# Attention backward on one core: dK and the transpose of dS from one product per chunk, in a pair of PSUM banks of their own

## The chip, the core and the metric

The kernel runs on one core of a Trainium2 chip. The metric is device time in microseconds (us) of one execution. Three executions of the kernel before took 1696.48, 1707.16 and 1713.74 us; the median, 1707.16 us, is the time to compare with. Engines are named as in the profile: PE is the matrix engine (PEld its weight loads), DVE the vector engine, ACT the scalar engine, POOL the general one, SP the queue that issues loads.

## The reference, cut to what matters

Two independent attention blocks A and B are computed, forward and backward, with bf16 inputs. For each block:

```
B, Sq, D = 8, 96, 640;  H, Sk, Dh = 32, 512, 128
q = (x @ wq).reshape(B, Sq, H, Dh).transpose(0, 2, 1, 3)
scores = einsum("bhqd,bhkd->bhqk", q, k_cache) * Dh ** -0.5
p = softmax(scores);  o = einsum("bhqk,bhkd->bhqd", p, v_cache)
out = o.transpose(0, 2, 1, 3).reshape(B, Sq, H * Dh) @ wo
```

The outputs are the two `out`, side by side, and the gradients of all ten inputs for a given `grad_out`: dx, dK, dV, dwq and dwo of each block. With dP = dO Vᵀ, the softmax's gradient is dS = P ∘ (dP − rowsum(O ∘ dO)), and from it dK = dSᵀ Q and dQ = dS K.

## The kernel before, in words

The unit of work is a chunk: one (block, head, batch) triple, of which there are 2 × 32 × 8 = 512. A chunk has 96 query rows and 512 keys, cut into KC = 4 pieces of 128 keys. Each chunk goes through stages that lie in different ticks, one new chunk per tick, so that a tick works on about seven chunks at once. Within a tick PE's work is written in this order:

- `c_s8`, first part (L340): dQ of an older chunk, four products with `dST_sb`, into the tile `x_ps`.
- `c_s8`, second part (L346): the four pieces of the younger chunk's `dS_sb`, 96 by 128 each, are transposed by products with the identity into `dst_ps` (bf16); DVE copies that to `dST_sb` (L348). The next tick's L340 reads it.
- `c_s7` (L432): dK, four products of the same pieces of `dS_sb` with Q (`Qnat_h`, 96 by 128 a batch), into `dK_ps` (f32, one bank); ACT copies it to `dK_sb` (L435).
- `c_s45`: O (L359) and the transpose of P (L365), into the same `x_ps` as dQ; ACT takes both O and dQ out at L375 and the transpose of P (`PT_sb`) at L378.
- `c_s4`: dV (L389), taken out by ACT (L392).
- `c_s6`: dP (L417) and the row sums (`dl_ps`, L419); DVE forms `dS_sb` from both (L421).
- Scores for a younger chunk (`S_ps`, L298), with the row maximum on DVE (`negm`, L300) and the exponential on ACT (`E_sb`, L310). On DVE `rinv` (L320) and on POOL `P_sb` (L329) follow.
- For some chunks K is transposed on PE (`kT_ps`, L285) and copied by DVE (`KT_pe`, L287); for the others by a DMA.

Once a head come larger pieces: the transposes of wo and wq (`woT_ps` L210, `wqT_ps` L216), Q and dO (`q_ps`, L243), their transposes (`n_ps`, L258, copied to `Qnat_h` and `dOnat_h`), the transposes of O and dQ (`nat_ps`, L455, copied to `Onat` on ACT and `dQnat` on DVE), dwo (L470), dwq (L490). Once in a group of about six heads come the output projections `o_ps` (L512), 12 pairs of sums.

All PSUM tiles come from one pool of eight banks (`ps`, L648), handed out in turn under the tag "bank". A tile's first product waits until the engine that emptied the bank's former tile has finished. The order of instructions on each engine is made when the program is built: the emitter sorts by tick and slot, and a scheduler then orders each engine's instructions by readiness and priority. Every engine works through its own list in order.

Of the kernel before, what the change touches and what calls it, by code (L numbers as in the profile page):

```python
# [7 lines left out]
ACT = mybir.ActivationFunctionType  # L8
ALU = mybir.AluOpType
AX = mybir.AxisListType  # L10
F32 = mybir.dt.float32
BF16 = mybir.dt.bfloat16
PSUM = bass.MemoryType.PSUM
# [33 lines left out]
EV = dict(pB0="act", pB1="dve", pC00="act", pC01="act", pC10="act", pC11="dve", pD0="dve", pD1="dve", qA0="act", qA1="dve", qB0="act", qB1="dve", qD="dve", gU="act")  # L47
# [3 lines left out]
SLOTS = dict(LOAD=0, S2A=5, S2B=5.5, S1=6, S8=10, S7=20, S5=30, S4=40, S6=50, S3A=52, S3B=53, S5B=54, HEAD=SL_HEAD, GRP=SL_GRP)  # L51


def build_block(tc, em, tick0, blk, x, kc, vc, wq, wo, g_all, out_all, dx, dk, dv, dwq, dwo, ident, ones, pools, HG=6, first=True, groups=None):
    nc = tc.nc
    B, Sq, D = x.shape
    _, H, Sk, Dh = kc.shape
# [5 lines left out]
    KC = Sk // 128  # L63
    NB = 2
    assert B % NB == 0 and H % 2 == 0
    scale = float(Dh) ** -0.5
# [8 lines left out]
    t0 = 0  # L75
    while t0 < T:
        w = 512 if T - t0 >= 512 else (256 if T - t0 >= 256 else (128 if T - t0 >= 128 else T - t0))
# [3 lines left out]
    c0 = 0  # L81
    while c0 < D:
        w = 512 if D - c0 >= 512 else (256 if D - c0 >= 256 else 128)
# [12 lines left out]
    const, ps, kvp, wk, hd, hst, grp = (pools[k] for k in ("const", "ps", "kvp", "wk", "hd", "hst", "grp"))  # L96

    def bank(shape, dt, name):
        return ps.tile(shape, dt, name=name, tag="bank")

    S = {}
    G = {}
    SB = {}
    HS = pools["HS"]
    CS = pools["CS"]
# [16 lines left out]
    def setup_T(which_, t):  # L122
        def f():
            key = "xT" if which_ == 0 else "gT"
            if t == 0:
                S[key] = const.tile([128, DC, T], BF16, name=key, bufs=1)
            dst = S[key]
            if first:
                tmp = S["x_nat" if which_ == 0 else "g_nat"][:, t, :]
            else:  # L130
                tmp = S.pop(("tmp", which_, t))
            pt = bank([128, DC * 128], BF16, "tp_ps")
            for c in range(DC):
                nc.tensor.transpose(pt[:, c * 128:(c + 1) * 128], tmp[:, c * 128:(c + 1) * 128], ident[:])
            evac("act" if first and t % 2 == 0 else "dve", dst[:, :, t * 128:(t + 1) * 128], pt[:].rearrange("p (c k) -> p c k", k=128))
        return f
# [18 lines left out]
    def evac(eng, dst, src, sc=None):  # L155
        if eng == "act":
            nc.scalar.activation(dst, src, ACT.Identity, scale=(1.0 if sc is None else sc))
        else:
            if sc is None:
                nc.vector.tensor_copy(dst, src)  # L160
            else:
                nc.vector.tensor_scalar(dst, src, float(sc), None, op0=ALU.mult)
# [84 lines left out]
    def pD(h, which):  # L247
        def f():
            st = HS[(blk, h)]
            src = st["QT_h"] if which == 0 else st["dOT_h"]  # L250
            dst = hd.tile([Sq, B * 128], BF16, name="Qnat_h" if which == 0 else "dOnat_h")
            st["Qnat_h" if which == 0 else "dOnat_h"] = dst
            for b0 in range(0, B, 8):
                nb = min(8, B - b0)
                n_ps = bank([Sq, 8 * 128], BF16, "n_ps")
                for i in range(nb):
                    b = b0 + i
                    nc.tensor.transpose(n_ps[:, i * 128:(i + 1) * 128], src[:, b * Sq:(b + 1) * Sq], ident[:])  # L258
                evac(EV["pD%d" % which], dst[:, b0 * 128:(b0 + nb) * 128], n_ps[:, 0:nb * 128])
        return f  # L260

    def c_ld(h, b, n, bufs):
# [67 lines left out]
                st["P_sb"] = P_sb  # L330
        return f

    def c_s8(tick, k8, k7):
        def f():
            XP[tick] = bank([128, 1024], BF16, "x_ps")
            if k8 is not None:
                st = CS[(k8[0], k8[1], k8[2])]
                dQT_ps = XP[tick][:, 2 * Sq:4 * Sq].bitcast(F32)
                for c in range(KC):
                    nc.tensor.matmul(dQT_ps, st["K_sb"][:, c, :], st["dST_sb"][:, c * Sq:(c + 1) * Sq], start=(c == 0), stop=(c == KC - 1))  # L340
                del CS[(k8[0], k8[1], k8[2])]
            if k7 is not None:
                st7 = CS[(k7[0], k7[1], k7[2])]
                dST_ps = bank([128, KC * Sq], BF16, "dst_ps")
                for c in range(KC):
                    nc.tensor.transpose(dST_ps[:, c * Sq:(c + 1) * Sq], st7["dS_sb"][:, c * 128:(c + 1) * 128], ident[0:Sq, 0:Sq])  # L346
                dST_sb = wk.tile([128, KC * Sq], BF16, name="dST_sb", bufs=2)
                nc.vector.tensor_copy(dST_sb[:], dST_ps[:])  # L348
                st7["dST_sb"] = dST_sb
        return f  # L350

    def c_s45(tick, k8, k5, k4):
# [72 lines left out]
    def c_s7(h, b):  # L425
        def f():
            st = CS[(blk, h, b)]
            hs = HS[(blk, h)]
            dS_sb = st["dS_sb"]
            dK_ps = bank([128, KC * 128], F32, "dK_ps")  # L430
            for c in range(KC):
                nc.tensor.matmul(dK_ps[:, c * 128:(c + 1) * 128], dS_sb[:, c * 128:(c + 1) * 128], hs["Qnat_h"][:, b * 128:(b + 1) * 128], start=True, stop=True)  # L432
            if b % 2 == 0:
                SB[(blk, h, b // 2, "k")] = wk.tile([128, 2, KC * 128], BF16, name="dK_sb", bufs=3)
            nc.scalar.activation(SB[(blk, h, b // 2, "k")][:, b % 2], dK_ps[:], ACT.Identity, scale=1.0)  # L435
        return f

    def qA(h, which):
# [113 lines left out]
    for g in range(NG):  # L552
        h0 = GH0[g]
        for hh in range(groups[g]):
            h = h0 + hh
# [56 lines left out]
        for i, (which, t, gi) in enumerate(subs):  # L612
            if which == 0:
                tk = cLg + OFF["s5"] + 2 + (i * gs0) // n_out
            else:
                tk = cLg + OFF["s8"] + 2 + gs0 - 3 + ((i - n_out) * gs1) // n_out
# [6 lines left out]
def _kernel_impl(tc, A_x, A_k_cache, A_v_cache, A_wq, A_wo, B_x, B_k_cache, B_v_cache, B_wq, B_wo, grad_out,  # L623
           out_0, out_1, out_2, out_3, out_4, out_5, out_6, out_7, out_8, out_9, out_10, HG=6, slots=None, off=None, hk=None, ev=None, gspread=None, groupsA=None, groupsB=(6, 6, 6, 6, 6, 2)):
    global GSPREAD0, GSPREAD1
    nc = tc.nc
    if slots:
        SLOTS.update(slots)
    if off:
        OFF.update(off)  # L630
    if hk:
        HK.update(hk)
    if ev:
        EV.update(ev)
    if gspread:
        GSPREAD0, GSPREAD1 = gspread
    with ExitStack() as ctx:
        P = lambda **kw: ctx.enter_context(tc.tile_pool(**kw))
        cst = P(name="gconst", bufs=1)
        ident = cst.tile([128, 128], BF16, name="ident")  # L640
        make_identity(nc, ident[:])
        ones = cst.tile([128, 1], BF16, name="ones")
        nc.vector.memset(ones[:], 1.0)
        warm = cst.tile([128, 128], BF16, name="warm")
        nc.vector.memset(warm[:], 1.0)
        pools = dict(
            const=P(name="const", bufs=1),
            ps=P(name="ps", bufs=8, space=PSUM),  # L648
            kvp=P(name="kv", bufs=11),
            wk=P(name="wk", bufs=3),  # L650
            hd=P(name="hd", bufs=2),
            hst=P(name="hst", bufs=HG + 2),
            grp=P(name="grp", bufs=1),
            stp=P(name="stp", bufs=5),
        )
        warm_ps = pools["ps"].tile([128, 128], F32, name="warm_ps", tag="bank")
        for _ in range(32):
            nc.tensor.matmul(warm_ps[:], warm[:], warm[:], start=True, stop=True)
        pools["SX"] = {}
        pools["XP"] = {}  # L660
        pools["OD"] = pools["const"].tile([128, 2, HG + 2, A_x.shape[0] * A_x.shape[1]], BF16, name="OD", bufs=1)
        pools["HS"] = {}
        pools["CS"] = {}
        em = Emitter()
        t_next = 13
        for blk, args in enumerate(((A_x, A_k_cache, A_v_cache, A_wq, A_wo, grad_out, out_0, out_1, out_2, out_3, out_4, out_5),
                                    (B_x, B_k_cache, B_v_cache, B_wq, B_wo, grad_out, out_0, out_6, out_7, out_8, out_9, out_10))):
            H_ = args[1].shape[1]
            if blk == 0:
                grps = groupsA  # L670
            else:
                grps = groupsB
            t_next = build_block(tc, em, t_next, blk, *args, ident, ones, pools, HG=HG, first=(blk == 0), groups=grps)
        for tk, (k8, k7, k5, k4) in pools["SX"].items():
            em.add(tk, SLOTS["S8"], pools["c_s8"](tk, k8, k7))
            em.add(tk, SLOTS["S5"], pools["c_s45"](tk, k8, k5, k4))
        em.run()

# [63 lines left out]
```

## Time and profile before

| what | value |
|---|---|
| executions, us | 1696.48, 1707.16, 1713.74 |
| profiled execution, first to last instruction (span), us | 1699.8 |
| PE busy | 1675.7 us, 99% |
| DVE busy | 1329.8 us, 78% |
| ACT busy | 1405.2 us, 83% |
| POOL busy | 1040.3 us, 61% |
| granted PE clock, mean | 0.998 |
| `dst_ps` transposes (L346) | 2048 |
| dK products (L432) | 2048 |
| copy of `dst_ps` by DVE (L348) | 512, 346 ns each |
| copy of `dK_ps` by ACT (L435) | 512, 590 ns each |

The profile gives the span; the time of the profiled execution, which has what lies around the span in it too, is not recorded apart from the three above. The span is 7.4 us under their median. A busy time is the union of an engine's instructions; products overlap each other, so a row's mean duration is longer than the step from one product's start to the next one's. In the timeline "x4" joins four instructions, and the difference of two rows' starts is the time that PE really gave to the first.

### The profile page before, as it was taken

What the parts mean: (1) busy time and instruction counts of PE and PEld (TensorE: products, weight loads), DVE (VectorE), ACT (ScalarE), POOL (GpSimd) and SP (SyncE); (2) the same over time, 40 slices, a digit from 0 to 9 for tenths busy, and PEclk for the clock granted to TensorE, in tenths of its full rate; (3) what the DMA queues carried; (4) which work ended last, traced back from release to release, by engine and by line L of the source; (5) the groups of instructions that cost most, each with busy time, mean ns of one, the idle gap of its engine ahead of it and who ended that gap; (6) DMA issues with size and microseconds to landing.
All of it is one profiled execution on the core that took longest, in us unless ns stands there. A gap on an engine that the chain in (4) does not pass through costs nothing.

```text
span 1699.8 us, 56567 instructions
## 1 busy us (share of the span) xinstructions
PE 1675.7 (99%) x22024; PEld 1343.8 (79%) x22024; DVE 1329.8 (78%) x3052; ACT 1405.2 (83%) x3518; POOL 1040.3 (61%) x1747
## 2 busy tenths in 40 slices
PE   8999999999999999999999999999999999999999
PEld 7877778778778778777778877887788778778876
DVE  6887678878788878787778876787788778878877
ACT  6998889869869869878768998897799679878975
POOL 3676567646647647656566764675576557656754
PEclk9999999999999999999999999999999999999999
DMA  9999999999999999999999999999899989999994
GB/s 256 252 259 250 258 225 260 262 242 243 262 221 252 268 238 259 225 251 237 281 256 269 273 270 248 238 289 248 218 261 276 237 221 261 281 217 240 263 247 141
DMA packets 600429, 423.05 MB, mean 249 GB/s; under 512 B 419360, under 2 KB 557984, under 8 KB 600160
## 3 DMA queue, kind: packets, MB, share of 16 engines
q1 hardware_dynamic: 546576, 242.08, 72.2%
q0 software_dynamic: 53584, 177.35, 32.7%
q8 instruction: 173, 2.83, 0.7%
q14 instruction: 96, 0.79, 0.2%
HBM read 161.09 MB, written 159.12 MB: 188 GB/s over the span
## 4 chain that ended last, share of the span: by engine, by line
PE 89%; DMA 4%; ACT 3%; issue 1%; DVE 1%; POOL 0%; SPq 0%; DVEq 0%; ACTq 0%; POOLq 0%
PE q_ps L243 12%; PE o_ps L512 12%; PE dwo_ps L470 6%; PE dV_ps L389 6%; PE dK_ps L432 6%; PE S_ps L298 6%; PE dP_ps L417 6%; PE dwq_ps L490 6%; PE x_ps L340 5%; PE x_ps L365 5%; PE dst_ps L346 5%; PE x_ps L359 5%; PE kT_ps L285 3%; PE n_ps L258 3%; PE nat_ps L455 2%; DMA VT<-V_sb 1%
## 5 line engine op out<-in xcount | busy, mean ns | idle before, releaser
L329 POOL TENSOR_SCALAR P_sb<-E_sb,rinv 96x512 bf16<-96x512 bf16 x512 | 352.6, 689 | 567.8 <-DVE rinv L320 559.2
L310 ACT ACTIVATE E_sb<-S_ps,negm 96x512 bf16<-96x512 f32 x512 | 351.0, 686 | 187.6 <-DVE negm L300 181.9
L421 DVE SCALAR_TENSOR_TENSOR dS_sb<-dP_ps,dl_ps,P_sb 96x512 bf16<-96x512 f32 x512 | 382.1, 746 | 60.9 <-PE dl_ps L419 54.6
L300 DVE TENSOR_REDUCE negm<-S_ps 96x1 f32<-96x512 f32 x512 | 347.6, 679 | 50.9 <-PE S_ps L298 46.6
L435 ACT ACTIVATE dK_sb<-dK_ps 128x512 bf16<-128x512 f32 x512 | 302.1, 590 | 63.4 <-PE dK_ps L432 56.5
L392 ACT ACTIVATE dV_sb<-dV_ps 128x512 bf16<-128x512 f32 x512 | 311.6, 609 | 0.0
L378 ACT ACTIVATE PT_sb<-x_ps 128x384 bf16<-128x384 bf16 x512 | 253.1, 494 | 0.0
L512 PEld LDWEIGHTS <-OD 128*128 128x128 bf16 x1536 | 132.2, 98 | 100.4 <-issue 1.0
L398 POOL DMA_DIRECT2D out_dram<-dV_sb x256 | 194.9, 761 | 11.8 <-issue 8.6
L398 POOL DMA_DIRECT2D out_dram<-dK_sb x256 | 195.0, 762 | 9.1 <-issue 4.4
L389 PE MATMUL dV_ps<-dOnat_h,P_sb 96*128 96x128 bf16 x2048 | 198.2, 219 | 0.8 <-DVE dOnat_h L160 0.6
L417 PE MATMUL dP_ps<-VT,dOT_h 128*96 128x512 bf16 x512 | 195.4, 382 | 3.0 <-DMA VT<-V_sb 3.0
L432 PE MATMUL dK_ps<-Qnat_h,dS_sb 96*128 96x128 bf16 x2048 | 198.1, 219 | 0.1
L407 POOL TENSOR_TENSOR prod<-OD,dOT_h 128x96 bf16<-128x96 bf16 x512 | 184.2, 360 | 13.8 <-ACT OD L375 12.6
L348 DVE COPY dST_sb<-dst_ps 128x384 bf16<-128x384 bf16 x512 | 177.1, 346 | 10.5 <-PE dst_ps L346 10.3
L365 PE MATMUL x_ps<-ident,P_sb 96*128 96x96 bf16 x2048 | 172.0, 205 | 0.8 <-POOL P_sb L329 0.3
L359 PE MATMUL x_ps<-PT_sb,V_sb 128*128 128x96 bf16 x2048 | 172.3, 206 | 0.2 <-ACT PT_sb L378 0.2
L346 PE MATMUL dst_ps<-ident,dS_sb 96*128 96x96 bf16 x2048 | 172.3, 206 | 0.2 <-DVE dS_sb L421 0.2
L340 PE MATMUL x_ps<-dST_sb,K_sb 128*128 128x96 bf16 x2048 | 171.0, 206 | 1.3 <-ACT dK_sb L435 0.8
L375 ACT ACTIVATE OD<-x_ps 128x192 bf16<-128x192 f32 (+1 forms) x515 | 167.9, 326 | 3.9 <-PE x_ps L340 3.9
L320 DVE RECIPROCAL rinv<-rowsum 96x1 f32<-96x1 f32 x512 | 79.9, 156 | 106.0 <-ACT E_sb L310 100.4
L340 PEld LDWEIGHTS <-K_sb 128*128 128x128 bf16 x2048 | 131.1, 98 | 25.1 <-issue 1.6
(84 smaller groups left out, 3744.4 us busy)
## 6 DMA issues: line engine op xcount, KB each, us to landing
out_dram<-dV_sb POOLq DMA_DIRECT2D x256, 256.0 KB, 5.2
out_dram<-dK_sb POOLq DMA_DIRECT2D x256, 256.0 KB, 5.3
K_sb<-in_A_k_cache_dram SPq DMA_DIRECT2D x128, 256.0 KB, 5.3
V_sb<-in_A_v_cache_dram SPq DMA_DIRECT2D x128, 256.0 KB, 5.2
K_sb<-in_B_k_cache_dram SPq DMA_DIRECT2D x128, 256.0 KB, 5.0
V_sb<-in_B_v_cache_dram SPq DMA_DIRECT2D x128, 256.0 KB, 4.9
out_dram<-dwo_sb POOLq DMA_DIRECT2D x63, 160.0 KB, 4.8
out_dram<-dwq_sb POOLq DMA_DIRECT2D x31, 320.0 KB, 6.1
```

The lines of the kernel that those rows point to most:

```text
L300: nc.vector.tensor_reduce(negm[:], S_ps[:], axis=AX.X, op=ALU.max, negate=True)
L310: nc.scalar.activation(E_sb[:], st["S_ps"][:], ACT.Exp, bias=st["negm"][:], scale=1.0, accum_out=rowsum[:])
L329: pinned(nc.gpsimd.tensor_scalar(P_sb[:], st["E_sb"][:], st["rinv"][:], 0.0, op0=ALU.mult, op1=ALU.add))
L340: nc.tensor.matmul(dQT_ps, st["K_sb"][:, c, :], st["dST_sb"][:, c * Sq:(c + 1) * Sq], start=(c == 0), stop=(c == KC - 1))
L389: nc.tensor.matmul(dV_ps[:, c * 128:(c + 1) * 128], P_sb[:, c * 128:(c + 1) * 128], hs["dOnat_h"][:, b * 128:(b + 1) * 128], start=True, s ...
L392: nc.scalar.activation(SB[(blk, h, b // 2, "v")][:, b % 2], dV_ps[:], ACT.Identity, scale=1.0)
L398: pinned(nc.gpsimd.dma_start(dst[b - 1:b + 1, h].rearrange("b (p c) d -> p b (c d)", c=KC), SB.pop((blk, h, b // 2, which))[:]))
L417: nc.tensor.matmul(dP_ps[:], hs["dOT_h"][:, tok], st["VT"], start=True, stop=True)
L421: nc.vector.scalar_tensor_tensor(dS_sb[:], dP_ps[:], dl_ps[:, 0:1], st["P_sb"][:], op0=ALU.subtract, op1=ALU.mult)
L432: nc.tensor.matmul(dK_ps[:, c * 128:(c + 1) * 128], dS_sb[:, c * 128:(c + 1) * 128], hs["Qnat_h"][:, b * 128:(b + 1) * 128], start=True, s ...
L435: nc.scalar.activation(SB[(blk, h, b // 2, "k")][:, b % 2], dK_ps[:], ACT.Identity, scale=1.0)
L512: nc.tensor.matmul(o_ps[:], src[:, t * 128:(t + 1) * 128], rhs, start=(hh == 0), stop=(hh == groups[g] - 1))
```

## The change

The transpose of dS is no longer a product of its own. Q and a 96 by 96 identity stand side by side in a new constant tile `QN`, so that one product of a piece of `dS_sb` with 224 columns gives both dK's piece (128 columns) and the transpose's (96). Even and odd batches share one identity: Q of the even batch, identity, Q of the odd batch. `QN` has two slots, used by heads in turn, and the identities are written once at the start. The result is f32 and needs two banks: a tile `dk_pair` in a pool slot of its own, one buffer of two banks; the other tiles have six banks in place of eight. DVE copies the transpose from the pair (f32 now, in four runs) to `dST_sb`, then ACT copies dK's four runs to `dK_sb`. In the program as built, ACT's copy waits for DVE's. The copy of Q into `QN` (`pD`) writes runs of 128 columns.

```
-            if k7 is not None:
-                dST_ps = bank([128, KC * Sq], BF16, "dst_ps")
-                for c in range(KC):
-                    nc.tensor.transpose(dST_ps[:, c * Sq:(c + 1) * Sq], st7["dS_sb"][:, c * 128:(c + 1) * 128], ident[0:Sq, 0:Sq])
-                dST_sb = wk.tile([128, KC * Sq], BF16, name="dST_sb", bufs=2)
-                nc.vector.tensor_copy(dST_sb[:], dST_ps[:])
-                st7["dST_sb"] = dST_sb
...
-            dK_ps = bank([128, KC * 128], F32, "dK_ps")
+            rhs = nat_view(pools["QN"], hs["nslot"], b)
+            pair = ps.tile([128, 2, 512], F32, name="dk_pair", tag="pair", bufs=1)
             for c in range(KC):
-                nc.tensor.matmul(dK_ps[:, c * 128:(c + 1) * 128], dS_sb[:, c * 128:(c + 1) * 128], hs["Qnat_h"][:, b * 128:(b + 1) * 128], start=True, stop=True)
+                nc.tensor.matmul(pair[:, c // 2, (c % 2) * (128 + Sq):(c % 2 + 1) * (128 + Sq)], dS_sb[:, c * 128:(c + 1) * 128], rhs, start=True, stop=True)
+            k0, t0 = (0, 128) if b % 2 == 0 else (Sq, 0)
+            dST_sb = wk.tile([128, KC * Sq], BF16, name="dST_sb", bufs=2)
+            nc.vector.tensor_copy(in4(dST_sb[:]), pair_part(pair, t0, Sq))
+            st["dST_sb"] = dST_sb
...
-            nc.scalar.activation(SB[(blk, h, b // 2, "k")][:, b % 2], dK_ps[:], ACT.Identity, scale=1.0)
+            nc.scalar.activation(in4(SB[(blk, h, b // 2, "k")][:, b % 2]), pair_part(pair, k0, 128), ACT.Identity, scale=1.0)
...
-            ps=P(name="ps", bufs=8, space=PSUM),
+            ps=P(name="ps", bufs=6, space=PSUM),
...
+    def nat_view(t, slot, b):
+        return t[:, slot, b // 2, 0:128 + Sq] if b % 2 == 0 else t[:, slot, b // 2, 128:256 + Sq]
+
+    def pair_part(pair, c0, w):
+        return pair[:, :, 0:2 * (128 + Sq)].rearrange("p a (c n) -> p a c n", c=2)[:, :, :, c0:c0 + w]
...
+            if which == 0:
+                st["nslot"] = (blk * H + h) % 2
+                v = pools["QN"][:, st["nslot"], 0, 0:128]
+                v = bass.AP(v.tensor, v.offset, [v.ap[0], (256 + Sq, B // 2), (128 + Sq, 2), (1, 128)])
+                evac(EV["pD0"], v, n_ps[:].rearrange("p (a c n) -> p a c n", c=2, n=128))
...
+        pools["QN"] = pools["const"].tile([sq, 2, nb // 2, 256 + sq], BF16, name="QN", bufs=1)
+        for s_ in range(2):
+            for p_ in range(nb // 2):
+                nc.vector.tensor_copy(pools["QN"][:, s_, p_, 128:128 + sq], ident[0:sq, 0:sq])
```

The order as built also changes. Before, ACT's list within a tick is E, dK, O/dQ, PT, dV in 449 of the 512 ticks. After, dK's copy stands third in 141 of the ticks (E, O/dQ, dK, PT, dV), fourth in 217 (E, O/dQ, PT, dK, dV) and fifth or later in about 145; in 63 of these it stands behind a head's copy as well (`Onat`, `woT_h` or `dwo_sb`). On PE the new product stands where the transposes stood in 421 ticks, behind O and the transpose of P in 41, behind dV in 22 and behind dP in 20.

More of the change, by code (lines that the diff above doesn't have):

```diff
@@ L99, in bank, with in4 @@
         return ps.tile(shape, dt, name=name, tag="bank")
+    def nat_view(t, slot, b):
+        return t[:, slot, b // 2, 0:128 + Sq] if b % 2 == 0 else t[:, slot, b // 2, 128:256 + Sq]
+    def pair_part(pair, c0, w):
+        return pair[:, :, 0:2 * (128 + Sq)].rearrange("p a (c n) -> p a c n", c=2)[:, :, :, c0:c0 + w]
+    def in4(ap):
+        return ap.rearrange("p (a c n) -> p a c n", a=2, c=2)
     S = {}
@@ L250, in f @@
             src = st["QT_h"] if which == 0 else st["dOT_h"]
[L251 to L259, printed above, removed]
+            n_ps = bank([Sq, B * 128], BF16, "n_ps")
+            for b in range(B):
+                nc.tensor.transpose(n_ps[:, b * 128:(b + 1) * 128], src[:, b * Sq:(b + 1) * Sq], ident[:])
+            if which == 0:
[3 more added lines that the diff above has]
+                evac(EV["pD0"], v, n_ps[:].rearrange("p (a c n) -> p a c n", c=2, n=128))
+            else:
+                st["dOnat_h"] = hd.tile([Sq, B * 128], BF16, name="dOnat_h")
+                evac(EV["pD1"], st["dOnat_h"][:], n_ps[:])
         return f
@@ L331, in c_s3b, with c_s8 @@
         return f
-    def c_s8(tick, k8, k7):
+    def c_s8(tick, k8):
         def f():
@@ L341, in f @@
                 del CS[(k8[0], k8[1], k8[2])]
-            if k7 is not None:
-                st7 = CS[(k7[0], k7[1], k7[2])]
-                dST_ps = bank([128, KC * Sq], BF16, "dst_ps")
-                for c in range(KC):
-                    nc.tensor.transpose(dST_ps[:, c * Sq:(c + 1) * Sq], st7["dS_sb"][:, c * 128:(c + 1) * 128], ident[0:Sq, 0:Sq])
-                dST_sb = wk.tile([128, KC * Sq], BF16, name="dST_sb", bufs=2)
-                nc.vector.tensor_copy(dST_sb[:], dST_ps[:])
-                st7["dST_sb"] = dST_sb
         return f
@@ L663, in _kernel_impl @@
         pools["CS"] = {}
+        sq, nb = A_x.shape[1], A_x.shape[0]
+        pools["QN"] = pools["const"].tile([sq, 2, nb // 2, 256 + sq], BF16, name="QN", bufs=1)
+        for s_ in range(2):
+            for p_ in range(nb // 2):
+                nc.vector.tensor_copy(pools["QN"][:, s_, p_, 128:128 + sq], ident[0:sq, 0:sq])
         em = Emitter()
@@ L674, in _kernel_impl @@
         for tk, (k8, k7, k5, k4) in pools["SX"].items():
-            em.add(tk, SLOTS["S8"], pools["c_s8"](tk, k8, k7))
+            em.add(tk, SLOTS["S8"], pools["c_s8"](tk, k8))
             em.add(tk, SLOTS["S5"], pools["c_s45"](tk, k8, k5, k4))
```

## The prediction

> **What bounds the kernel now.** I read the page first, for the share of each engine.
>
> ```profile
> PE 1675.7 (99%) x22024; PEld 1343.8 (79%) x22024; DVE 1329.8 (78%) x3052; ACT 1405.2 (83%) x3518; POOL 1040.3 (61%) x1747
> ```
>
> PE is busy 99%, but its products overlap, so I took the timeline next and measured from start to start. The four rows below are one stretch of PE in a tick.
>
> ```profile
> 269.05 0.33 PE L340 MATMUL x_ps<-dST_sb,K_sb 128*128 128x96 bf16 x4
> 269.22 0.34 PE L346 MATMUL dst_ps<-ident,dS_sb 96*128 96x96 bf16 x4
> 269.39 0.39 PE L432 MATMUL dK_ps<-Qnat_h,dS_sb 96*128 96x128 bf16 x4
> 269.62 0.34 PE L359 MATMUL x_ps<-PT_sb,V_sb 128*128 128x96 bf16 x4
> ```
>
> Four products of 96 columns step by 0.17 us (42 ns each), four of 128 by 0.22 to 0.23 (55 ns each). There is no idle time between groups and no sign of the weight loads: PE streams columns. The next rows are five products of 256 columns in another stretch, 0.54 us for five, 108 ns each.
>
> ```profile
> 803.19 0.71 PE L243 MATMUL q_ps<-xT,wq_p 128*128 128x256 bf16 x5
> ...
> 803.73 0.71 PE L243 MATMUL q_ps<-gT,woT_h 128*128 128x256 bf16 x5
> ```
>
> Then the busy times by stage, one stretch per head. Columns: stretch, its length, busy us of PE, PEld, DVE, ACT, POOL, clock, DMA share, GB/s.
>
> ```profile
> 253.60:274.80 21.20, 21.13 (x306) 17.48 (x304) 18.00 (x42) 20.98 (x55) 14.98 (x26) 1.00 1.14 282
> 274.80:299.10 24.30, 24.18 (x338) 20.37 (x335) 19.98 (x45) 21.82 (x56) 17.18 (x29) 1.00 1.13 250
> 299.10:321.80 22.70, 22.64 (x319) 18.40 (x316) 18.16 (x43) 21.51 (x55) 16.64 (x28) 1.00 1.15 269
> 321.80:353.80 32.00, 32.00 (x396) 24.73 (x393) 24.09 (x55) 22.11 (x54) 16.26 (x27) 1.00 1.14 243
> ```
>
> This is what decides. The mean of 83% for ACT hides two kinds of heads. In heads with output projections (32 us) ACT and DVE have 8 to 10 us free. In light heads (21.2 and 22.7 us) ACT is busy 99% and 95%: PE and ACT bound them together. The lengths repeat every six heads with two light ones among them, so about 21 of 64 heads are light. Everything PE needs from ACT comes late there, and eight banks of slack have hidden it so far.
>
> **The change part by part.**
>
> PE. Removed per chunk: four transposes and four dK products, 269.22 to 269.62, 0.39 to 0.40 us. Added: four products of 224 columns. Between 55 ns at 128 and 108 ns at 256, a straight line gives 55 + 53 × 96/128 = 95 ns, 0.38 us. Gain 0.01 to 0.02 us × 512, about 6 us (5 to 10). The columns streamed are the same, 4 × (96 + 128) = 4 × 224; only the step over each product's columns, some 2 ns × 2048, is saved, and 2048 weight loads that cost nothing. This is the most that PE can give, since it does not wait now.
>
> Here a rule speaks against the row. The Trainium skill, "TensorE: Matmul & The Clock Gate", section "Back-to-back issue gap", says that in streams of weight loads and products a product of 128 columns costs about 81 ns and one of 512 about 131 ns. By that, two products would cost some 160 ns, one of 224 about 94 ns, and the change would be worth an estimated 140 us. The rows above step by 55 ns at 128 columns, so I go by the rows.
>
> DVE. The copy to `dST_sb` takes 346 ns from bf16; from f32 these are the nearest rows:
>
> ```profile
> L348 DVE COPY dST_sb<-dst_ps 128x384 bf16<-128x384 bf16 x512 | 177.1, 346 | 10.5 <-PE dst_ps L346 10.3 <-PE x_ps L365 0.2
> L160 DVE CAST dwo_sb<-dwo_ps 128x320 bf16<-128x320 f32 x64 | 30.8, 481 | 0.5
> L160 DVE CAST dOT_h<-q_ps 128x256 bf16<-128x256 f32 x64 | 26.6, 415 | 8.3 <-PE q_ps L243 8.3
> ```
>
> 64 columns more cost 66 ns, so 384 columns cost 481 + 66 = 547 ns, 0.20 us more. Over 512 that is 103 us of DVE, which has 370 us idle. Light heads: 18.0 + 8 × 0.2 = 19.6 of 21.2 us. Covered on the whole; the bounds are 0 and, were nothing of it covered in the 21 light heads, 21 × 1.6 = 34 us. DVE still has 1.6 us free in such a head, so I take a quarter, 9 us. Queued behind the longer copy are `rinv`, `dS_sb` and `negm`, for which POOL, PE and ACT wait.
>
> ACT. The copy of dK keeps its 512 columns (590 ns), now in four runs from two banks. No row has that; rows of one size with and without runs on DVE agree (`xT` 128x640 482 ns, `wqT_h` 128x640 478), so 0 is taken, and the spread of ACT's two 512-column copies (590 and 609 ns, 10 us over 512) is kept as the bound on both sides. What changes is the wait: this copy is now behind DVE's, and the next tick's product behind it, since the pair has one buffer. For the why, the Trainium skill, "PSUM — Partial Sum Buffer", section "PSUM bank collisions raise a hardware error", says that two engines may not access one bank at a time, reads included. No row of this trace shows it.
>
> The wait's price is walked in a light head. ACT there:
>
> ```profile
> 269.70 0.68 ACT L310 ACTIVATE E_sb<-S_ps,negm 96x512 bf16<-96x512 f32 x1
> ...
> 270.38 0.58 ACT L435 ACTIVATE dK_sb<-dK_ps 128x512 bf16<-128x512 f32 x1
> 270.86 0.32 ACT L375 ACTIVATE OD<-x_ps 128x192 bf16<-128x192 f32 x1
> 271.07 0.49 ACT L378 ACTIVATE PT_sb<-x_ps 128x384 bf16<-128x384 bf16 x1
> 271.44 0.60 ACT L392 ACTIVATE dV_sb<-dV_ps 128x512 bf16<-128x512 f32 x1
> 271.92 0.71 ACT L157 ACTIVATE woT_h<-woT_ps 128x640 bf16<-128x640 bf16 x1
> 272.50 0.70 ACT L310 ACTIVATE E_sb<-S_ps,negm 96x512 bf16<-96x512 f32 x1
> ```
>
> and PE in the tick after:
>
> ```profile
> 271.61 0.33 PE L340 MATMUL x_ps<-dST_sb,K_sb 128*128 128x96 bf16 x4
> 271.77 0.34 PE L346 MATMUL dst_ps<-ident,dS_sb 96*128 96x96 bf16 x4
> ```
>
> ACT's steps from start to start are 0.68, 0.48 (dK), 0.21, 0.37, 0.48, 0.58. The order as built puts dK last here. So O starts at 270.38, PT at 270.59, dV at 270.96, `woT_h` at 271.44 and ends 272.15, dK at 272.02 and ends 272.60. With six banks, dQ's `x_ps` has the bank that `woT_ps` had: PE wants it at 271.61 and gets it at 272.15, 0.54 late. The new product stands behind O and the transpose of P in this tick, so it is wanted 0.51 after dQ, 272.66 by then; dK is out at 272.60. The same walk two heads' copies earlier, with `Onat` (0.82) in place of `woT_h`, gives 0.3 to 0.4 us at the tick that begins at 264.05. If ACT slips no further, the second loss has the first in it; if it slips with PE, they add. So 0.55 to 0.9 us a light head, 12 to 19 us over 21; the score product, which with six banks waits for the copy of PT (270.59 + 0.49 = 271.08 against 270.76 in this tick), is inside the first and adds where the head's copies are elsewhere. I take 0.95 a light head, 20 us, and 0.2 for each of the other 43, 9 us. Bounds: nothing, if the waits only eat slack; and 1.5 us in every head, about 95 us, if each of two or three such waits costs its own time.
>
> The eight copies of the identity at the start are 96 columns each, while DVE waits 7.1 us for the first transposes: nothing. `pD`'s copy in runs: nothing, by the two rows of 640 columns. Loads, stores and POOL's list are the same.
>
> Sum: −6 + 9 + 20 + 9 = +32 us. The profiled span is 1699.8 us, 7.4 under the median of the runs; added to the median, 1707.2 + 32 = 1739 us.
>
> **The rivals.**
>
> *The waits are hidden, and PE's gain remains* (the other side). For it: the scheduler has moved the new product behind O, dV or dP in 83 ticks, and DVE and ACT have whole microseconds free in the 43 other heads. Against it: in light heads ACT has 0.22 us in 21.2. Price: 1707 − 6 = 1701, up to 1724 if half of my waits stay. It decides if light heads lose under 0.3 us each.
>
> *Lockstep.* The loop product, DVE's copy, ACT's copy, next product (0.55 + 0.55 + 0.6 us and queueing) and the loop scores, `negm`, E, PT, bank, scores both close every tick, and a light tick has 2.4 to 2.7 us. If a delay on one engine is passed on to the next and not caught up, light heads stretch by 2 to 4 us: 21 × 3 + 43 × 1 − 6 = +100, 1807 us. For it: ACT at 99%. Against it: three quarters of all time has slack on two engines.
>
> *The product does not stream.* Two 224-column results a bank, f32, read by two engines: if it stepped like one of 256 columns, 108 ns, PE would lose 13 × 2048 = 27 us, 1766 with the rest; nothing in the rows suggests it.
>
> **How the numbers follow.** My forecast (waits of 23 to 85 us net of the gain, 1724 to 1790): 0.58. Hidden, 1690 to 1724: 0.28. Lockstep and anything above 1790: 0.11. A gain over 1%, under 1690: 0.03, since PE can give only 10. The point is the forecast's 1739. The range leaves out about a tenth on each side: 1703 (hidden, the gain alone nearly whole) to 1790. One per cent, 17 us, is about what a measurement can tell from no change: faster 0.03, same 0.28, slower 0.69.
>
> **What would show it.** PE: four products of 224 columns stepping by 0.38 us; more than 0.40 and that term is wrong. DVE: the copy near 547 ns. Light heads: 22 to 23 us in place of 21.2, with PE waits on ACT before dQ, the scores and the pair; heavy heads unchanged at 32. If light heads stay at 21.2 or shorter, the waits were hidden and I am wrong; if heavy heads grow too, it is lockstep.

## The result and the profile after

After the change the kernel takes 1760.62 us (median of four runs, 1759.78 to 1761.83), before it 1703.21 us (median of four, 1696.48 to 1713.74). The ratio is 1.032, with a 95% interval of 1.0273 to 1.0366: 57 us slower. The profiled span grew from 1699.8 to 1758.0 us.

The page of the profile after, busy times and the shares of the chain that ended last:

```profile
PE 1701.4 (97%) x19976; PEld 1342.9 (76%) x19976; DVE 1432.0 (81%) x3060; ACT 1423.1 (81%) x3518; POOL 1028.9 (59%) x1747
...
PE 65%; ACT 21%; DVE 9%; issue 5%; DMA 0%; POOL 0%; ACTq 0%; SPq 0%; DVEq 0%; POOLq 0%
```

The chain of the kernel before:

```profile
PE 89%; DMA 4%; ACT 3%; issue 1%; DVE 1%; POOL 0%; SPq 0%; DVEq 0%; ACTq 0%; POOLq 0%
```

PE's "busy" fell only from 99% to 97% and looks harmless. The chain says more: before, 89% of it was PE; now it leaves PE for ACT and DVE in 30% of the span. PE has become an engine that is waited for by others and waits for them.

The same four heads as in the prediction (stretch, length, busy us of PE, PEld, DVE, ACT, POOL):

```profile
259.00:281.60 22.60, 21.76 (x275) 17.56 (x272) 19.66 (x42) 21.54 (x55) 14.89 (x26) 1.00 1.14 270
281.60:306.40 24.80, 24.35 (x304) 20.34 (x302) 21.45 (x45) 21.94 (x55) 17.04 (x29) 1.00 1.14 258
306.40:330.60 24.20, 23.35 (x287) 18.42 (x284) 19.78 (x43) 21.84 (x55) 16.48 (x28) 1.00 1.10 278
330.60:363.70 33.10, 32.54 (x365) 24.85 (x362) 25.55 (x55) 21.96 (x54) 16.04 (x27) 1.00 1.08 218
```

They were 21.2, 24.3, 22.7 and 32.0 us. The two light heads lost 1.4 and 1.5 us, the others 0.5 and 1.1. PE had 0.07 us without a product in the first of them before, and has 0.84 now.

The timeline where a score product is late (start, duration, engine, line, tiles; in brackets the idle time and what ended it). It shows rows of PE and ACT, and last the row maximum on DVE; the dots stand for rows left out:

```profile
264.71 0.55 PE L436 MATMUL dk_pair<-QN,dS_sb 96*128 96x224 bf16 x4
...
265.09 0.34 PE L362 MATMUL x_ps<-PT_sb,V_sb 128*128 128x96 bf16 x4
...
265.98 0.31 ACT L378 ACTIVATE OD<-x_ps 128x192 bf16<-128x192 f32 x1
...
266.19 0.48 ACT L381 ACTIVATE PT_sb<-x_ps 128x384 bf16<-128x384 bf16 x1
266.24 0.22 PE L262 MATMUL n_ps<-ident,dOT_h 128*96 128x128 bf16 x1
...
266.56 0.59 ACT L443 ACTIVATE dK_sb<-dk_pair 128x512 bf16<-128x512 f32 x1
266.72 0.38 PE L309 MATMUL S_ps<-KT,QT_h 128*96 128x512 bf16 x1 [0.27 <-ACT PT_sb L381]
...
267.13 0.69 DVE L311 TENSOR_REDUCE negm<-S_ps 96x1 f32<-96x512 f32 x1 [0.21 <-PE S_ps L309]
```

Four products of 224 columns take 0.38 us from 264.71 to 265.09, as forecast. But S_ps starts 0.48 us after the 128-column product ahead of it, which needs 0.055: 0.43 us of PE are lost until `PT_sb` has been copied out of the bank, and the row maximum behind S_ps, on DVE, waits too. The bracket shows only 0.27, since the end of a product is modelled late; steps between starts show it in full.

Taken over the whole trace in that way (each step from one product's start to the next one's, less what its columns need), PE lost 49 us before and 113 us after. A loss is put down here to the copy on another engine that ended last before the product. Of these 113 us, 30 stand before S_ps behind the copy of `PT_sb` (104 times) and 22 before other tiles behind the same copy; 12 before dQ's `x_ps` behind `Onat` or `woT_h`; and 13 before the new product, 4 of them behind dK's copy and 9 behind `dS_sb`. The rest is spread over many small waits, most of which were there before. Lost time grew by some 63 us; less some 6 us that the product saves, that is about the 58 us of the span.

The three groups that the change touched:

```profile
L443 ACT ACTIVATE dK_sb<-dk_pair 128x512 bf16<-128x512 f32 x512 | 307.7, 601 | 2.0 <-DVE dST_sb L439 1.9
L436 PE MATMUL dk_pair<-QN,dS_sb 96*128 96x224 bf16 x2048 | 280.9, 259 | 3.5 <-DVE dS_sb L424 1.3
L439 DVE CAST dST_sb<-dk_pair 128x384 bf16<-128x384 f32 x512 | 280.7, 548 | 29.7 <-PE dk_pair L436 20.9 <-PE dwo_ps L478 0.3
```

ACT stood 1.9 us in all at its new wait for DVE: the wait that the change adds in plain sight costs nothing on ACT.

### The profile page after: what moved, and what is told of

The parts are those of the page before. It is cut to its first block, busy times and chain, and to the rows that moved or that the text cites. A ratio compares the mean times of both kernels' runs of the same rounds, so it can differ in the third digit from the quotient of the medians.

```text
span 1758.0 us, 52467 instructions
## 1 busy us (share of the span) xinstructions
PE 1701.4 (97%) x19976; PEld 1342.9 (76%) x19976; DVE 1432.0 (81%) x3060; ACT 1423.1 (81%) x3518; POOL 1028.9 (59%) x1747
## 4 chain that ended last, share of the span: by engine, by line
PE 65%; ACT 21%; DVE 9%; issue 5%; DMA 0%; POOL 0%; ACTq 0%; SPq 0%; DVEq 0%; POOLq 0%
PE o_ps L520 11%; PE q_ps L252 10%; ACT E_sb L321 8%; PE dk_pair L436 6%; PE dwq_ps L498 6%; PE S_ps L309 5%; DVE negm L311 5%; PE dwo_ps L478 4%; ACT PT_sb L381 4%; PE dV_ps L392 4%; PE dP_ps L420 4%; ACT dK_sb L443 3%; PE x_ps L351 3%; PE x_ps L368 3%; PE x_ps L362 3%
## 5 line engine op out<-in xcount | busy, mean ns | idle before, releaser
L424 DVE SCALAR_TENSOR_TENSOR dS_sb<-dP_ps,dl_ps,P_sb 96x512 bf16<-96x512 f32 x512 | 381.4, 745 | 22.7 <-PE dl_ps L422 11.9
L443 ACT ACTIVATE dK_sb<-dk_pair 128x512 bf16<-128x512 f32 x512 | 307.7, 601 | 2.0 <-DVE dST_sb L439 1.9
L439 DVE CAST dST_sb<-dk_pair 128x384 bf16<-128x384 f32 x512 | 280.7, 548 | 29.7 <-PE dk_pair L436 20.9
L436 PE MATMUL dk_pair<-QN,dS_sb 96*128 96x224 bf16 x2048 | 280.9, 259 | 3.5 <-DVE dS_sb L424 1.3
L381 ACT ACTIVATE PT_sb<-x_ps 128x384 bf16<-128x384 bf16 x512 | 248.6, 486 | 0.0
L436 PEld LDWEIGHTS <-dS_sb 96*128 96x128 bf16 x2048 | 171.5, 97 | 14.4 <-DVE dS_sb L424 12.6
L368 PE MATMUL x_ps<-ident,P_sb 96*128 96x96 bf16 x2048 | 178.2, 205 | 0.3
L252 PE MATMUL q_ps<-gT,woT_h 128*128 128x512 bf16 (+1 forms) x640 | 136.8, 325 | 4.7 <-ACT PT_sb L381 3.9
```

The lines of the kernel that those rows point to most:

```text
L252: nc.tensor.matmul(q_ps[:], lhs(c), rhsT[:, c, t0:t0 + w], start=(c == 0), stop=(c == DC - 1))
L381: nc.scalar.activation(PT_sb[:], PT_ps, ACT.Identity, scale=1.0)
L424: nc.vector.scalar_tensor_tensor(dS_sb[:], dP_ps[:], dl_ps[:, 0:1], st["P_sb"][:], op0=ALU.subtract, op1=ALU.mult)
L436: nc.tensor.matmul(pair[:, c // 2, (c % 2) * (128 + Sq):(c % 2 + 1) * (128 + Sq)], dS_sb[:, c * 128:(c + 1) * 128], rhs, start=True, stop= ...
L443: nc.scalar.activation(in4(SB[(blk, h, b // 2, "k")][:, b % 2]), pair_part(pair, k0, 128), ACT.Identity, scale=1.0)
```

## The experiments

My theory after the result: the loss is bank shortage. The two products need two banks at a time as before, but those two are now set apart, and the tiles that go round on the other six meet a bank whose last reader, ACT, is late. The rivals: DVE's longer copy (T2), and the chain product, DVE's copy, ACT's copy, next product, through a pair with one buffer (T3).

**The split of the banks alone.** Before, with the banks of after.

```
-dST_ps = bank([128, KC * Sq], BF16, "dst_ps")
+dST_ps = ps.tile([128, KC * Sq], BF16, name="dst_ps", tag="dst", bufs=1)
...
-dK_ps = bank([128, KC * 128], F32, "dK_ps")
+dK_ps = ps.tile([128, KC * 128], F32, name="dK_ps", tag="dk", bufs=1)
...
-ps=P(name="ps", bufs=8, space=PSUM)
+ps=P(name="ps", bufs=6, space=PSUM)
```

> The products of before, with the banks of after: the transposes of dS and dK each have one bank of their own, and six banks are left for the rest. If the shortage of banks is what costs (the score product that waits for PT_sb is the largest wait of PE in the profile after), this lies near 1745 us, at least 1730. If the longer copy on DVE or the serial chain product, DVE's copy, ACT's copy, next product is the cause, neither is here, and it stays at 1700 to 1712.

Measured 1804.4 us, ratio 1.0589 (1.0547 to 1.0632). Neither the longer copy nor the chain is in it, and it loses 100 us, more than the whole change. So split banks can cost all of it, and something in the change has won some of it back. The waits of PE in this run (engine, tile, line, releaser: us, times, longest):

```profile
PE S_ps L298 <- ACT PT_sb L378: 30.4, 97, 0.5
PE dwq_ps L490 <- ACT PT_sb L378: 11.9, 28, 0.5
PE q_ps L243 <- ACT PT_sb L378: 9.1, 14, 0.9
```

All three wait for the copy of `PT_sb`; by steps from start to start PE loses 100 us in all behind that copy here, against 53 after the change. In the order as built, ACT's copy of dK stands ahead of that of `PT_sb` in practically every tick here (in 430 of them as E, dK, O/dQ), as it did before the change, and in 146 after it; it puts `PT_sb` off by its own step of 0.48 us.

**DVE's longer copy alone.** Before, with f32 transposes.

```
-dST_ps = bank([128, KC * Sq], BF16, "dst_ps")
+dST_ps = bank([128, KC * Sq], F32, "dst_ps")
...
-nc.tensor.transpose(dST_ps[:, c * Sq:(c + 1) * Sq], st7["dS_sb"][:, c * 128:(c + 1) * 128], ident[0:Sq, 0:Sq])
+nc.tensor.matmul(dST_ps[:, c * Sq:(c + 1) * Sq], st7["dS_sb"][:, c * 128:(c + 1) * 128], ident[0:Sq, 0:Sq], start=True, stop=True)
```

> Before with one change: the transposes of dS are f32 products with the identity, so that DVE's copy takes about 548 ns in place of 346; eight banks and the order of work as before. If DVE's longer copy costs, 1735 to 1760 us. If the banks or the chain do, under 1715.

Measured 1720.84 us, ratio 1.0106 (1.0049 to 1.0163): 16 us beside the 1704.44 of its own runs of before, just above the line drawn for the theory of banks and well under T2's. The copy took 547 ns. Its cost is real: PE waits for `dS_sb`, which now comes later; by steps from start to start it loses 16 us behind `dS_sb`, against 1 us before. First the copy's row, then one of PE's waits:

```profile
L348 DVE CAST dST_sb<-dst_ps 128x384 bf16<-128x384 f32 x512 | 279.9, 547 | 10.2 <-PE dst_ps L346 9.2
...
PE dst_ps L346 <- DVE dS_sb L421: 8.8, 22, 0.7
```

**The short copy in the changed kernel.**

```
-nc.vector.tensor_copy(in4(dST_sb[:]), pair_part(pair, t0, Sq))
+nc.vector.tensor_copy(in4(dST_sb[:]), pair_part(pair, t0, Sq // 2).bitcast(BF16))
```

> After with DVE's copy reading the transpose's first halves as bf16 (384 columns of bf16, about 346 ns, as before the change; the transpose that comes out is not dS's, so dQ, dwq and dx are left wrong). If banks are the cause, 1745 to 1758 us, a small gain. If DVE's copy is the cause, 1700 to 1720.

Measured 1785.61 us, ratio 1.0488 (1.0441 to 1.0535): slower than after with less work on DVE, which no theory expected. The order as built gave it away: with the shorter copy (median 344 ns) the scheduler puts dK's copy ahead of `PT_sb`'s in 347 ticks in place of 146, presumably since it takes dK as ready earlier. The run does not tell the price of the copy, but points at the order on ACT.

**dK's copy ahead of DVE's.** The two lines of `c_s7` that copy out of the pair exchanged.

> After with ACT's copy of dK ahead of DVE's copy of the transpose: the same two copies from the same pair, the chain in the other order. If banks are the cause, within 15 us of after (1745 to 1775). If ACT's wait for DVE is the cause, 1700 to 1725.

Measured 1854.07 us, ratio 1.0883 (1.0839 to 1.0927). A miss for all: turned round, the kernel takes 93 us more. DVE's copy now waits for ACT, which is late, and dQ for DVE (rows of the waits of PE):

```profile
PE x_ps L351 <- DVE dST_sb L442: 34.6, 57, 1.2
PE S_ps L309 <- ACT PT_sb L381: 10.5, 53, 0.5
```

The 93 us need not all be the chain's: the order on ACT changed along with it, and dK's copy stands ahead of `PT_sb`'s in nearly every tick here, as in the split of the banks alone, which took 1804.4 us. But dQ's wait for DVE is new. So T3's chain can cost time; whether it does in the order that the change chose, this run does not tell.

**A bank of its own for S_ps.** If the meeting of two tiles in one bank were the loss, to keep them apart would cure it.

```
-S_ps = bank([Sq, Sk], F32, "S_ps")
+S_ps = ps.tile([Sq, Sk], F32, name="S_ps", tag="s", bufs=1)
...
-ps=P(name="ps", bufs=6, space=PSUM)
+ps=P(name="ps", bufs=5, space=PSUM)
```

> After with one of its six banks kept for the score tile S_ps alone, five for the rest. In after, 104 score products wait for ACT's copy of PT_sb, whose x_ps had their bank, 30 us in all. If that meeting of two tiles in one bank is the loss, 1715 to 1740 us. If six banks are simply too few, the waits move to the other tiles on five banks, and this is at 1755 us or more.

Measured 1953.15 us, ratio 1.1445 (1.1373 to 1.1517). The waits moved to the next tiles in turn, and became larger:

```profile
PE n_ps L262 <- ACT PT_sb L381: 51.1, 97, 0.6
PE wqT_ps L225 <- ACT PT_sb L381: 15.4, 27, 0.6
PE dl_ps L422 <- ACT PT_sb L381: 12.5, 10, 1.5
```

Keeping S_ps apart cured nothing: another tile meets the late bank. The 190 us need not all be the missing bank's, for the order on ACT changed here too: dK's copy stands ahead of `PT_sb`'s in some 430 ticks, in place of 146.

**Seven banks in place of eight.** Before, `bufs=7`, nothing else.

> Before with seven banks in its pool, the eighth unused; nothing else changed. If the number of banks for tiles that go round in turn is what counts, this loses some 15 to 40 us (1718 to 1745); if only the special banks of the change cost, it stays at 1700 to 1712.

Measured 1747.26 us, ratio 1.0241 (1.0171 to 1.0311). One bank less, with nothing else edited and nearly the same order on ACT, costs 45 us. Eight banks hid the lateness of ACT and seven do not, which PE's waits before do not show: there it waits for nearly nothing.

**dK's copy late.** After, with ACT's copy of dK written behind that of `PT_sb`.

```
+st["pair"] = pair_part(pair, k0, 128)
...
+em.add(ct + OFF["s7"], 35, c_s7k(h, b))
```

(`c_s7k` holds the copy; slot 35 lies behind the slot of `PT_sb`'s copy, 30.)

> After with ACT's copy of dK put behind that of PT_sb in every tick (in after it stands ahead of it in 146 ticks and delays it by 0.48 us there); the wait of the next product for the pair can only grow. If the score product's wait for PT_sb is the main loss, some 8 to 20 us are won: 1740 to 1753. If the chain product, DVE's copy, ACT's copy, next product is the main loss, this is slower than after: 1765 to 1785.

Measured 1735.43 us, ratio 1.0193 (1.0106 to 1.0281): 25 us faster than after (22 by the ratios; 8 to 20 were expected), though the pair is set free later. T3 falls as the main loss. Who waited for the tile `PT_sb`, after:

```profile
  PE S_ps L309: 15.3, 67
  PE q_ps L252: 7.4, 14
  PE o_ps L520: 2.5, 7
```

and with dK's copy late:

```profile
  PE q_ps L252: 4.6, 12
...
  PE S_ps L309: 0.3, 1
  PE o_ps L525: 0.3, 2
```

The bracketed idle time before S_ps is gone. By steps from start to start 15 of the 30 us there remain; behind the copy of `PT_sb` in all, 32 of 53.

**The same with the short copy.** The edits of the last run and of the short copy together.

> The same with DVE's copy at the old 346 ns (the first halves read as bf16; dQ, dwq and dx are left wrong). The run with the short copy alone took 1785.6 us, but there ACT's copy of dK stood ahead of PT_sb's in 347 ticks. If that order made it slow, this comes to 1735 to 1750; what it then lacks to the run beside it with the long copy is DVE's share (5 to 15 us). If the short copy itself is slow in some way, it stays near 1785.

Measured 1726.76 us, ratio 1.0135 (1.0064 to 1.0205), where the short copy without the late dK took 1785.61. The order made that run slow. Beside the long copy with late dK the short one is worth 9 us, a difference that the two intervals do not part from nothing.

**Two products or one, with as many banks and the same order on ACT.** The split banks with two products, and the one product in its pair, each with the order of ACT fixed to `PT_sb`, dK, dV in every tick (by `pinned(...)` around the copies of `PT_sb` and dK, for the one product of dV too).

> Two separate products and the banks of after (transposes of dS and dK one bank each, six for the rest; 1804 us with dK's copy ahead of PT_sb's in 430 ticks), now with ACT's order fixed: the copies of PT_sb, then dK, in every tick. If the order of ACT is what made that run slow, it falls by 40 to 80 us, to 1725 to 1765, and the same banks with the one product (1735 us with late dK) differ from it by under 20 us. If two products are slow in themselves on six banks, it stays above 1785.

> The one product with ACT's order fixed to PT_sb, dK, dV in every tick (1735 us with dK behind PT_sb, where 144 ticks still had dK last). If the next product's wait for the pair matters, this is faster, 1715 to 1730; if the wait of S_ps for PT_sb alone does, 1728 to 1742. ACT could also stand at DVE's copy, then 1745 or more.

Measured 1738.29 us for two products, ratio 1.0211 (1.0167 to 1.0255), and 1738.36 us for one, ratio 1.0212 (1.0175 to 1.0249). In both kernels ACT's order is E, O/dQ, `PT_sb`, dK, dV in all but a few ticks. The order on PE is not quite alike: the one product stands behind O or further back in some 45 ticks, the two products in hardly any.

With as many banks and the same order on ACT the one product is worth nothing, to within some 10 us. That DVE's longer copy takes what PE saves is likely (6 us and some 9), but these two runs do not show the parts.

The order is worth far more: two products on split banks took 1804.4 us with dK's copy ahead and take 1738.3 with it behind, 66 us less.

Two of the same four heads, first with two products, then with one:

```profile
251.40:273.10 21.70, 21.23 (x306) 17.59 (x305) 18.51 (x42) 21.22 (x55) 14.84 (x26) 1.00 1.13 254
273.10:297.80 24.70, 24.47 (x337) 20.47 (x336) 20.19 (x46) 22.05 (x55) 17.04 (x29) 1.00 1.14 276
```

```profile
253.10:275.20 22.10, 21.59 (x272) 17.60 (x271) 19.91 (x42) 21.29 (x55) 14.81 (x26) 1.00 1.11 270
275.20:299.70 24.50, 24.40 (x305) 20.42 (x303) 21.76 (x46) 22.15 (x56) 17.02 (x29) 1.00 1.13 264
```

In the light head, where DVE goes from 18.5 to 19.9 us, one product loses 0.4 us; in the next it wins 0.2. In the run with late dK, dK's place behind dV in 144 ticks cost nothing that shows: fixed ahead of dV (1738.36 us) it is no faster.

**The order alone, on eight and seven banks.** Before, and before with seven banks, with dK's copy behind `PT_sb`'s (the same edit).

> Before, eight banks, with only dK's copy put behind PT_sb's on ACT. With eight banks PE waits for neither, so by the theory of banks this changes nothing: 1695 to 1712. If the order of ACT's copies is worth something by itself, 1675 to 1690, or above 1720 if dK's bank is then late.

> Before with seven banks and dK's copy behind PT_sb's on ACT, in place of 1747 us with seven banks and dK's copy ahead. PT_sb's copy and with it x_ps's bank come 0.48 us earlier, but dK's bank 0.5 us later. Of the 45 us lost on seven banks, 13 stand at waits of S_ps for PT_sb and 25 at waits for dK's copy: if the order only moves the wait, 1735 to 1760; if PT_sb is the one that counts, 1715 to 1735.

Measured 1707.42 us on eight, ratio 1.001 (0.9977 to 1.0043), and 1751.84 us on seven, ratio 1.0299 (1.026 to 1.0338). On eight banks the order of ACT's copies is free. So the run on eight banks and the one of two products on split banks, both with dK's copy behind `PT_sb`'s, differ by their edits in the banks alone: 1707.4 and 1738.3 us. The 31 us between them are the price of the banks (2.1% against before itself).

On seven the order only moves the wait. By steps from start to start, with the steps at `q_ps` and `o_ps` left out (records of some of their products are missing from this trace), PE's losses behind dK's copy fall from 24 to 9 us, but those behind `PT_sb`'s grow from 17 to 22 and those behind DVE's copy `KT_pe` from 2 to 16. In these runs the order pays only where dK has a bank of its own.

No kernel of these beats the one before.

## Why the prediction was right, and where it was off

The time, 1760.6 us, lies 22 us above the forecast, in the forecast's own band of 1724 to 1790 and in the stated range of 1703 to 1790; slower had 0.69. The sum was +32 us and is +57. The ranges are wide, and the upper end of the band does not quite follow from its terms: waits of 85 us less the gain of 6 give 1786.

- PE's term was right. The products step by 95 ns, and the saving is about 6 us. No weight load showed itself. By the step of 81 ns at 128 columns that the Trainium skill gives ("TensorE: Matmul & The Clock Gate", "Back-to-back issue gap") the change would have won, by the prediction's estimate. The rows decide.
- DVE's term was right in the duration, 547 ns forecast and 548 measured. Its size fits: 9 us forecast, 9 us between the long and the short copy with late dK (the two intervals overlap), 16 us when it is put alone into the kernel before. That 9 meets 9 is in part luck, since the quarter behind it was a choice.
- ACT's copy of dK from four runs in two banks: 601 ns after 590, 6 us over 512 copies, inside the bound of 10.
- The waits were mis-sized: 29 us forecast, and some 54 by what the other terms leave of the 63 us of lost time, if DVE's copy takes its 9 here too. The mechanism was right, that the banks come from an ACT which is late. But the walk went by dQ's tile and the pair, and took the score product's wait for `PT_sb` to be "inside the first"; it is the main one, 30 us before S_ps and 22 before other tiles, against 13 at the pair. The walked losses are there: `Onat` 20 times with 0.36 us each (0.3 to 0.4 forecast), `woT_h` 21 times with 0.24 (0.54 forecast): 0.60 us together, where 0.55 to 0.9 was walked for a light head.
- No term of the sum was for the order on ACT, which the scheduler makes anew with each edit. It is some 20 of the 57 us.
- The term of 0.2 us for each of the other 43 heads failed most. From the dP product at one head's start to that of the next head, the 20 heads of under 23.2 us grew by 27 us together, as the terms for light heads say (20 and 9, less some 2 of PE's gain). The 43 others grew by 32 us, where 9 less some 4 was forecast.
- "Heavy heads unchanged at 32" was wrong: 33.1 us. They have the same tiles and more of them, and the copy of `PT_sb` holds back S_ps, dwq's and the projections' products there as well, however much free time ACT has on the whole. By the prediction's own sign ("if heavy heads grow too, it is lockstep") this speaks for lockstep in part; but the two light heads shown stretched by 1.4 and 1.5 us, not by 2 to 4.
- The wait that the diff shows, ACT behind DVE, cost 1.9 us.

What the runs show in its place, as a sum of ratios: six banks for the rest, with dK's copy fixed behind that of `PT_sb` on ACT, 2.1% (36 us); one product for two, 0.0%; the order on ACT that the scheduler made of the change, 1.1% (3.2% less 2.1%, some 20 us). The hidden-waits rival fell; the lockstep rival was too large at 1807 us, but the last link of its second loop (scores, `negm`, E, `PT_sb`, bank, scores), the score product's wait for the bank that `PT_sb` is copied from, is the largest wait in the trace; the rival of a product that does not stream fell.

Open: how the 36 us divide between fewer banks and banks set apart. With the same order on ACT, seven banks that all go round cost more than six and two set apart (3.0% against 2.1%). One product with eight banks for the rest would need ten, so it was not tried.

## What to carry to other kernels

Before a change takes banks from a pool, try the kernel with a pool one smaller: an engine that never waits can have no buffer to spare. Where an engine in order empties several banks, rank its copies by who waits next for each bank, and look at the order as built, not at the source: a cheaper instruction can make a slower kernel by changing the order. Merging two products into one with the same columns saves next to nothing where the rows step by columns alone, as here (some 6 us of 1700), and what matters is then the banks and the copies behind it.

## What was not expected of the hardware

- A copy by DVE of four f32 runs that lie in two banks costs no more than one run in one bank: 548 ns against 547 for 384 columns. ACT's costs 601 against 590 for 512.
- Products with a weight load each step by their columns, with no sign of the load: 42 ns at 96 columns, 55 at 128, 95 at 224, 108 at 256.
- One bank of eight, unused, cost 2.4%.
